# TensorE's products with wq and w3 written as hardware loops of eight turns, in a gated mix of cached attention and an MLP

## The chip, the cores and the metric

The metric is the time of one execution on the device, in microseconds (us), as a median over runs. Lower is better.

## The reference

For two tokens (batch 2, sequence length 1, width D = 1024) it computes `g * a + (1 - g) * b`:

```python
g = sigmoid((x * gate_w).sum(-1, keepdims=True))
# a: attention of one query over a cache of 16384 keys, 32 heads of width 128
q = (x @ wq).reshape(B, 1, 32, 128).transpose(0, 2, 1, 3)
p = softmax(einsum("bhqd,bhkd->bhqk", q, k_cache) * 128 ** -0.5)
a = einsum("bhqk,bhkd->bhqd", p, v_cache).transpose(0, 2, 1, 3).reshape(B, 1, 4096) @ wo
# b: an MLP block; hs is a token-shifted gelu(layernorm(x) @ w1), times w2.
# With one position every shifted copy is zeros; the kernel multiplies zeros with w2.
x1 = x + hs
b = x1 + gelu(layernorm(x1) @ w3) @ w4
```

All operands are bf16. wq is 1024 x 4096, w3 is 1024 x 3584, w4 is 3584 x 1024. The two caches are 2 x 32 x 16384 x 128 each, and make nearly all of the bytes.

## The kernel before

**Planning.** Nothing is issued while the program is written down. `_Plan` (L24) collects for each engine a list of operations with their waits; `add` (L43) appends an operation and, with `sig`, counts the engine's semaphore up by one; `dma` (L52) appends a load. `emit` (L78) then writes each list out in order. It can write a stretch of the list as a hardware loop (`Fori`, L100): the attention part, 32 rounds, becomes 16 turns of two rounds on PE, DVE and ACT. In that loop the value that a wait compares with depends on the turn and is worked out in a register (L72), and one operation per round, the scaled output on DVE (L704), writes to an address from a register.

**Memory.** `ring` has five slots of 128 partitions x 16384 bf16. wq takes slots 0 and 1, w2 slot 2, w3 slots 3 and 4, w4 again 0 and 1 (L352). Round n of the attention takes K into slots 2 and 3 or 3 and 4 (L353), and V into 0 and 1. `queue_load` (L304) lists the loads in a fixed order; `pump` (L307) puts a load on SP's list once its slots have been released, and the load waits for the semaphore values that the release names. SP works its list in order: a small first part of w3, wq, w2, the rest of w3, w4, K of round 0, V of round 0, and so on. `release` (L320) marks a slot free behind an event.

**The start, on PE.** Eight transposes of x and gate_w; the products with wq (L603 to L608): for each of eight blocks of 128 rows (`kc`) 32 products, one for each head, of a 128x128 weight block with a moving operand of two columns, accumulated in bank 1. The first product of a bank clears (`start`), the last of the eight closes. Then four products that spread q (L614), the gate, the products with w2 as rows (L510), `hs_columns`, the layer norm (in turns with DVE and POOL), the products with w3 (L477), the GELU on DVE and ACT, and the products with w4 as rows (L510). Then the loop of the attention, and the products with wo.

**The products with w3.** `dense_stage` (L468) is called eight times (L561), each time with one block `kl` of 128 rows: 28 products of a 128x128 weight block, whose columns lie 28 elements apart (`cols`), with two columns of the normed x. They add up in a zeroed part of bank 5. After the block with which all columns of a slot have been used, the stage releases that slot: slot 3 after the fifth block, slot 4 after the eighth. K of round 0 needs slots 2 and 3, K of round 1 slots 3 and 4.

**What follows from the order.** w4's load waits for the release of wq's slots, K of round 0 for the release of w2's slot and of w3's first, V of round 0 for the release of w4's. Each matmul is a weight load and a product on PE, two instructions, which the text calls a pair.

## Time and profile before

| | us |
|---|---|
| median of three runs | 1324.38 |
| lowest and highest | 1324.28, 1324.6 |
| the profiled execution | 1324.34 |
| its span, first to last instruction | 1323.0 |
| PE busy | 794.4 (60%) |
| DVE busy | 659.9 (50%) |
| TensorE clock granted, mean | 0.78 |

A profile is one execution as the hardware recorded it. The page gives busy times by engine, the span in 40 slices, the DMA queues, the chain of work that ended last, and the costliest groups of instructions. The views behind it are answers to questions about the same record: a timeline of a stretch, the instructions of one line of the code, the waits, the DMA issues. A row of the timeline has start, duration, engine, line, operation, what it writes from what, a count where several are merged, and in brackets how long the engine sat idle before it and what ended that. "issue" stands for a wait that the profile cannot name. SPq is a DMA issue by SP; PEldq and DVEq are instructions that the sequencers of PE and DVE carry out themselves. In the page's part on DMA issues stand KB, and the time from the issue to the landing of the last byte.

### The profile page before, as it was taken

The page shows a single profiled execution, that of the slowest core. Times are in us where ns is not written, and L with a number is a line of the kernel's source. Part 1 is how long each engine was busy: PE and PEld are TensorE (multiplying, and loading weights), DVE is VectorE, ACT ScalarE, POOL GpSimd, SP SyncE. Part 2 cuts the span into 40 slices and gives each one's busy share as a digit, 9 for nine tenths or more (in the row PEclk, how much of TensorE's full clock was granted, in tenths as well). Part 3 has the DMA queues.
Part 4 walks back from the last instruction along what each step waited for, and adds up shares of the span by engine and source line. Part 5 has one row for each costly group of instructions (what it writes and reads, how often), then busy time and mean ns, then how long its engine had stood idle before and what let it go on. Part 6 is the DMA issues. An engine that isn't in the chain of part 4 may idle for free.

```text
span 1323.0 us, 12314 instructions
## 1 busy us (share of the span) xinstructions
PE 794.4 (60%) x5235; PEld 337.7 (26%) x5235; DVE 659.9 (50%) x527; ACT 46.5 (4%) x101; POOL 23.5 (2%) x110
## 2 busy tenths in 40 slices
PE   1655567656556765655676565577565557756557
PEld 1622222212222222222222222222222222222223
DVE  0254446655444665544466554446655445665444
ACT  0000000000000000000000000000000000000000
POOL 3000000000000000000000000000000000000000
PEclk9977778786777877678787767878776787877678
DMA  9999999999999999999999999999999999999998
GB/s 417 433 423 435 436 432 432 436 432 440 428 434 438 428 434 438 430 434 436 430 438 432 430 438 432 430 440 430 430 440 430 430 440 430 430 440 430 430 440 367
DMA packets 11114, 570.60 MB, mean 431 GB/s; under 512 B 1232, under 2 KB 1756, under 8 KB 2015
## 3 DMA queue, kind: packets, MB, share of 16 engines
q1 hardware_dynamic: 11080, 570.43, 99.7%
q8 instruction: 8, 0.13, 0.0%
q14 instruction: 4, 0.02, 0.0%
q10 hardware_dynamic: 22, 0.01, 0.0%
HBM read 570.44 MB, written 0.00 MB: 431 GB/s over the span
## 4 chain that ended last, share of the span: by engine, by line
DMA 69%; PE 24%; DVE 6%; issue 1%; SPq 0%; POOL 0%
DMA ring<-in_A_k_cache_dram 65%; PE ps L654 23%; DVE ring L648 6%; DMA ring<-in_A_wo_dram 2%; DMA ring<-in_A_wq_dram 2%; PE ps L477 1%; PE ps L605 1%; DVE hsd L544 0%; PE ps L510 0%; PE ps L401 0%; SPq L334 0%; PE ps L729 0%; POOL mv L442 0%; DVE orow L763 0%; DVE q_f L617 0%
## 5 line engine op out<-in xcount | busy, mean ns | idle before, releaser
L654 PE MATMUL ps<-ring,Z 128*128 128x512 bf16 x2048 | 534.3, 420 | 375.9 <-DVE ring L648 374.6
L648 DVE STREAM_TRANSPOSE ring<-ring 128x2048 f32<-128x2048 f32 x256 | 565.2, 2274 | 264.6 <-DMA ring<-in_A_k_cache_dram 264.6
L654 PEld LDWEIGHTS ps<-ring,Z 128*128 128x128 bf16 x2048 | 204.2, 104 | 693.2 <-issue 459.3
L690 PE MATMUL ps<-ring,PT_sb 128*32 128x512 bf16 x2048 | 177.4, 523 | 4.3 <-DVE recip L681 3.9
L704 DVE SCALAR_TENSOR_TENSOR OT_sb<-ps,gT,recip 128x2 f32 x32 | 7.0, 220 | 213.0 <-PE ps L701 213.0
L690 PEld LDWEIGHTS ps<-ring,PT_sb 128*32 128x32 bf16 x2048 | 69.6, 126 | 98.4 <-issue 81.7
L675 ACT ACTIVATE P_sb<-ps,negm 128x512 bf16<-128x512 f32 x32 | 22.0, 687 | 995.5 <-DVE negm L673 995.5
L664 DVE TENSOR_REDUCE rA<-ps 128x1 f32<-128x512 f32 x32 | 22.1, 692 | 64.1 <-PE ps L654 64.1
L679 PE MATMUL ps<-rowsum,hsel 128*128 128x1 f32 x128 | 23.9, 291 | 38.0 <-ACT P_sb L675 38.0
L677 DVE STREAM_TRANSPOSE PT_sb<-P_sb 128x512 bf16<-128x512 bf16 x32 | 22.8, 711 | 27.1 <-ACT P_sb L675 27.1
L635 POOL TENSOR_TENSOR Z<-q_f,mask 128x8 bf16<-128x8 f32 x64 | 12.3, 227 | 1204.0 <-PE ps L654 1204.0
L679 PEld LDWEIGHTS ps<-rowsum,hsel 128*128 128x128 f32 x128 | 21.2, 235 | 40.7 <-ACT P_sb L675 40.7
L666 PE MATMUL ps<-ident,rmax_bf 128*1 128x128 bf16 x32 | 6.9, 217 | 33.1 <-DVE rmax_bf L665 33.1
L699 ACT ACTIVATE acc_sb<-ps 128x512 bf16<-128x512 f32 x32 | 19.1, 597 | 208.3 <-PE ps L690 208.3
L701 PE MATMUL ps<-dsel,acc_sb 128*128 128x2 bf16 x128 | 8.1, 167 | 22.5 <-ACT acc_sb L699 22.5
L605 PE MATMUL ps<-xT_bf,ring 128*128 128x2 bf16 x256 | 7.1, 165 | 18.4 <-DMA ring<-in_A_wq_dram 14.1
L477 PE MATMUL ps<-xn_bf,ring 128*128 128x2 bf16 x224 | 14.3, 202 | 1.4 <-DVE xn_bf L444 1.4
L701 PEld LDWEIGHTS ps<-dsel,acc_sb 128*128 128x128 bf16 x128 | 5.3, 96 | 38.3 <-ACT acc_sb L699 38.3
L666 PEld LDWEIGHTS ps<-ident,rmax_bf 128*1 128x1 bf16 x32 | 2.5, 79 | 48.9 <-DVE rmax_bf L665 48.9
L477 PEld LDWEIGHTS ps<-xn_bf,ring 128*128 128x128 bf16 x224 | 14.3, 162 | 1.4 <-issue 1.4
L667 DVE TENSOR_REDUCE m_sb<-ps 1x2 bf16<-1x128 bf16 x32 | 8.9, 279 | 9.9 <-PE ps L666 9.9
L673 DVE TENSOR_SCALAR negm<-ps,cAB 128x1 f32<-128x1 f32 x32 | 8.9, 277 | 9.2 <-PE ps L670 9.2
(99 smaller groups left out, 90.1 us busy)
## 6 DMA issues: line engine op xcount, KB each, us to landing
ring<-in_B_w_dram SPq DMA_DIRECT2D x1, 7168.0 KB, 26.4
ring<-in_B_w_dram SPq DMA_DIRECT2D x1, 6272.0 KB, 43.6
ring<-in_A_wo_dram SPq DMA_DIRECT2D x1, 4096.0 KB, 38.5
ring<-in_B_w_dram SPq DMA_DIRECT2D x1, 2048.0 KB, 28.1
ring<-in_A_wo_dram SPq DMA_DIRECT2D x1, 2048.0 KB, 22.7
ring<-in_A_wo_dram SPq DMA_DIRECT2D x1, 1024.0 KB, 24.8
ring<-in_B_w_dram SPq DMA_DIRECT2D x1, 896.0 KB, 4.6
ring<-in_A_k_cache_dram SPq DMA_DIRECT2D x32, 26.8
```

The costliest lines, as they stand in the source:

```text
L477: fn = lambda e, nb=nb, kl=kl: e.matmul(out_ps[:, nb, :], lhsT=cols(wv, kl, nb, nout), rhs=rhs_of(kl), start=False, stop=True, skip_group_ ...
L605: ev = pl.add("pe", lambda e, h=h, kc=kc: e.matmul(q_ps[:, h, :], lhsT=wv[:, kc, h * Dh:(h + 1) * Dh], rhs=xT_bf[:, kc, :], start=(kc == 0 ...
L635: ev = pl.add("pool", lambda e, hp=hp: e.tensor_tensor(Z[:, :, ZO:ZO + P].rearrange("p t (i c) -> p t i c", c=32)[:, :, 2 * hp:2 * hp + 2, ...
L648: return pl.add("dve", lambda e: e.transpose(ap, ap), waits=(arrived(("k", n)),), sig=True)
L654: ev = pl.add("pe", lambda e, bp=bp: e.matmul(S_ps[:, 0:NCOL], lhsT=Z[:, bp, ZO - 2 * u:ZO - 2 * u + P], rhs=kv[:, :, bp // 2, :, bp % 2], ...
L664: e1 = pl.add("dve", lambda e: e.tensor_reduce(rA[:, :], S_ps[:, 0:NCOL], axis=AX.X, op=ALU.max), waits=(ev_S[n],), sig=True)
L675: e7 = pl.add("act", lambda e: e.activation(P_sb[:, :], S_ps[:, 0:NCOL], ACT.Exp, bias=negm[:, 0:1], scale=scale, accum_out=rowsum[:, 0:1] ...
L677: e8 = pl.add("dve", lambda e: e.transpose(PT_sb[:, :], P_sb[:, :]), waits=(e7,), sig=True)
L679: e9 = pl.add("pe", lambda e, hp=hp: e.matmul(l_ps[:, hp:hp + 1], lhsT=hsel[:, hp, :], rhs=rowsum[:, 0:1], start=True, stop=True, skip_gro ...
L690: ev = pl.add("pe", lambda e, jj=jj, cg=cg: e.matmul(acc_ps[32 * cg:32 * cg + 32, 0:512], lhsT=PT_sb[:, 32 * jj:32 * jj + 32], rhs=vv[:, 4 ...
L699: e1 = pl.add("act", lambda e: e.activation(acc_sb[:, :], acc_ps[:, 0:512], ACT.Copy), waits=(ev_pv,), sig=True)
L701: e2 = pl.add("pe", lambda e, w=w: e.matmul(oT_ps, lhsT=acc_sb[:, w * P:(w + 1) * P], rhs=dsel[:, w, :], start=(w == 0), stop=(w == 3)), w ...
```

## The change

`_Plan` gets a method `turns`, which appends a hardware loop as one entry of an engine's list. Its waits stand ahead of the loop. In the body stand the given operations, which get the turn `i`, and the last of them counts the engine's semaphore up by one each turn; the event that others wait for is the value after the last turn.

```diff
+    def turns(self, eng, count, fns, waits=()):
+        sem = self.esem[eng]
+
+        def fn(e):
+            with e.Fori(0, count) as i:
+                for f in fns:
+                    ins = f(e, i)
+                ins.then_inc(sem, 1)
+
+        self.cnt[eng] += count
+        ev = _Ev(sem, self.cnt[eng])
+        self.ops[eng].append((self._merge(waits), fn, None, 1, False))
+        return ev
```

The products with wq become one such loop: eight turns (over `kc`) of 32 products. The addresses of the weight block and of the moving operand come from a register. As no turn is the first any more in the code, none clears: bank 1's 64 columns are zeroed by DVE before.

```diff
-        for kc in range(NBD):
-            for h in range(H):
-                ev = pl.add("pe", lambda e, h=h, kc=kc: e.matmul(
-                    q_ps[:, h, :], lhsT=wv[:, kc, h * Dh:(h + 1) * Dh], rhs=xT_bf[:, kc, :], start=(kc == 0 and h == 0),
-                    stop=(kc == NBD - 1), skip_group_check=True),
-                    waits=(arrived(key), ev_xT_bf) if h == 0 else (), sig=(h == H - 1))
+        ev_q0 = pl.add("dve", lambda e: e.memset(banks[1][:, 0:H * 2], 0.0), sig=True)
+        ev = pl.turns("pe", NBD, [lambda e, i, h=h: e.matmul(
+            q_ps[:, h, :], lhsT=wv[:, bass.ds(i, 1), h * Dh:(h + 1) * Dh].rearrange("p o d -> p (o d)"),
+            rhs=xT_bf[:, bass.ds(i, 1), :].rearrange("p o b -> p (o b)"), start=False, stop=True, skip_group_check=True)
+            for h in range(H)], waits=(arrived(key), ev_xT_bf, ev_q0))
```

The products with w3 become one loop of eight turns of 28 products. `dense_stage` is called once and releases both slots of w3 behind the last turn.

```diff
-                ev_arr = arrived(key)
-                ev = None
-                first = True
-                for nb in range(nout):
-                    for kl in kls:
-                        lastmm = (nb == nout - 1 and kl == kls[-1])
-                        fn = lambda e, nb=nb, kl=kl: e.matmul(
-                            out_ps[:, nb, :], lhsT=cols(wv, kl, nb, nout), rhs=rhs_of(kl),
-                            start=False, stop=True, skip_group_check=True)
...
-                for j, slot in enumerate(slots_of[key]):
-                    if kls[-1] == _cdiv(min(nkw * width, SLOT * (j + 1)), width) - 1:
-                        release(key, ev, (slot,))
+                fns = [lambda e, i, nb=nb: e.matmul(
+                    out_ps[:, nb, :], lhsT=wv[:, bass.ds(i, 1), :].rearrange("p o (q r) -> p (o q) r", r=nout)[:, :, nb],
+                    rhs=rhs_sb[:, bass.ds(i, 1), :].rearrange("p o b -> p (o b)"), start=False, stop=True, skip_group_check=True)
+                    for nb in range(nout)]
+                ev = pl.turns("pe", nkw, fns, waits=(arrived(key), evd[rhs_key]) + b5_waits())
+                release(key, ev)
...
-        put([dense_stage(key, [kl], NBD, NBF, h3_ps, lambda kc: xn_bf[:, kc, :], "xn2", "h3", F) for kl in range(NBD)], key)
+        put([dense_stage(key, NBD, NBF, h3_ps, xn_bf, "xn2", "h3", F)], key)
```

`b5_waits` gathers the waits that `pe_b5` put ahead of a product into bank 5.

## The prediction

> **What bounds the kernel now.** I read the head of the page and its DMA part first, then the DMA issues, then the chain of waits and the timeline of the first 112 us, and last the rows of the instructions that a sequencer carries out itself.

> ```profile
> span 1323.0 us, 12314 instructions
> DMA  9999999999999999999999999999999999999998
> q1 hardware_dynamic: 11080, 570.43, 99.7%
> HBM read 570.44 MB, written 0.00 MB: 431 GB/s over the span
> ring<-in_B_w_dram SPq DMA_DIRECT2D x1, 7168.0 KB, 26.4
> ring<-in_B_w_dram SPq DMA_DIRECT2D x1, 6272.0 KB, 43.6
> ring<-in_B_w_dram SPq DMA_DIRECT2D x1, 896.0 KB, 4.6
> ```

> The 16 DMA engines work 99.7% of the span. So the time is bytes over 431 GB/s, plus every microsecond in which SP has no load queued. PE matters only through the ring slots that it frees: an earlier free slot is worth nothing while loads are queued, a later one costs all of its lateness beyond the queued work. The place to look at is the start, where the weights pass through the slots:

> ```profile
> 24.93 5.81 PEld L605 LDWEIGHTS ps<-xT_bf,ring 128*128 128x128 bf16 x215 [14.18 <-DMA ring<-in_A_wq_dram]
> 24.94 5.87 PE L605 MATMUL ps<-xT_bf,ring 128*128 128x2 bf16 x214 [14.10 <-DMA ring<-in_A_wq_dram]
> 35.15 1.26 PE L605 MATMUL ps<-xT_bf,ring 128*128 128x2 bf16 x42 [4.34 <-issue]
> 36.44 0.33 SPq L334 DMA_DIRECT2D ring<-in_B_w_dram  x1
> 47.34 14.33 PE L477 MATMUL ps<-xn_bf,ring 128*128 128x2 bf16 x224 [1.35 <-DVE xn_bf L444]
> 56.38 0.33 SPq L361 DMA_DIRECT2D ring<-in_A_k_cache_dram  x1
> 63.77 5.80 PE L510 MATMUL ps<-ring,GT_bf 128*2 128x256 bf16 x112 [2.11 <-DVE GT_bf L462]
> 69.62 0.33 SPq L365 DMA_DIRECT2D ring<-in_A_v_cache_dram  x1
> ```

> Here columns are start, duration, engine, line. wq's products take 24.94 to 36.41, 11.47 us: 7.1 of work and 4.34 in which PE waits for nothing that the profile shows. Their end lets SP issue w4 (36.44). w4 lands 26.4 us later, at 62.8. Its 7168 KB (7.34 MB) need 17.0 us at 431 GB/s, so w3 landed and the queue would have run dry at 62.8 - 17.0 = 45.8. w3's products start 47.34 - 36.41 = 10.9 after the end of wq's and take 14.33; after 140 of 224 SP issues the first K load (56.38). The small load of 896 KB lands after 4.6 us, of which 2.1 are bytes: from an issue to the first bytes 2.5 us. So K's bytes could flow from 58.9, and w4 keeps the engines busy until 62.8: slack 3.9 us. For w4's issue it is 45.8 - 2.5 - 36.4 = 6.9 us.

> **The change, part by part.** The products, their shapes and their bytes stay. In code, 256 and 224 pairs of LDWEIGHTS and MATMUL become 32 and 28, each run eight times. Removed is the 4.34 us gap, if it is what it looks like, waiting for code: one packet of the instruction queue falls into it.

> ```profile
> DMA packets 98, 3.51 MB, mean 438 GB/s; under 512 B 16, under 2 KB 16, under 8 KB 16
> q8 instruction: 1, 0.02, 0.7%
> ```

> (DMA view of 28 to 36 us.) Added are, per turn, the loop's own instructions and, per product, the making of a register address. The trace has both kinds in the main loop: first all such instructions by line, then one back edge.

> ```profile
> L72 PEldq ALU_OP  x416: 32/32/42, 84.5 to 1308.6; - x139
> L72 PEldq FUSED_REGOPS  x48: 37/37/42, 84.4 to 1266.5; - x48
> L72 DVEq ALU_OP  x224: 40/40/52, 102.5 to 1311.3; - x112
> L704 DVEq FUSED_REGOPS  x32: 71/73/81, 111.9 to 1311.4; - x32
> L704 DVE SCALAR_TENSOR_TENSOR OT_sb<-ps,gT,recip x32: 218/220/221, 112.1 to 1311.5; 128x2 f32 x32
> ...
> L100 PEldq ALU_OP  x1: 32/32/32, 150.2 to 150.2; - x1
> L100 PEldq COMPARE_BRANCH  x1: 247/247/247, 150.3 to 150.3; - x1
> L100 PEldq FUSED_REGOPS  x1: 50/50/50, 150.6 to 150.6; - x1
> ```

> A q behind the engine marks its sequencer (ns min/median/max). *Per turn*: from 150.2 to the end of the last, 150.6 + 0.05: 0.45 us.

> *Per product*: at L704 each of 32 operations with a register address has a FUSED_REGOPS of its own, in both halves of the body, so I count one for each of the 32 or 28 weight addresses of a turn (the moving operand's is the same all turn and is made once). What one takes from its sequencer, with the hand-over:

> ```profile
> 43.05 0.05 issue
> 84.39 0.12 issue
> ...
> 111.55 0.25 PE L701 MATMUL ps<-dsel,acc_sb 128*128 128x2 bf16 x4 [0.70 <-ACT acc_sb L699]
> 112.06 0.22 DVE L704 SCALAR_TENSOR_TENSOR OT_sb<-ps,gT,recip 128x2 f32 x1 [6.54 <-PE ps L701]
> ...
> L72 PEldq ALU_OP  x2: 32/32/32, 123.1 to 123.2; - x2
> ```

> The first two are pieces of the chain between the end of a DVE operation and the start of PE's: 0.05 us plain, 0.12 with a 42 ns register instruction between, so 0.07 for that one. On DVE, from PE's end (111.80) to the operation with the address (112.06) pass 0.26 us for two register instructions and the hand-overs. Take off 0.05, and 0.21 is 0.105 each; PE's sequencer does the same ALU_OP in 32 ns where DVE's takes 40 (both at L72), so 0.085. Two register instructions with a group of products between them start 0.1 apart. That bounds the register part between 0.085 and 0.11. The pair itself took 5.87 us / 214 = 0.027 in wq and 14.33/224 = 0.064 in w3, and overlaps in part. **I take p = 0.12 us per product**, between 0.085 (all overlapped) and 0.11 + 0.027 = 0.14 (none).

> W, wq's products: 256 x 0.12 + 8 x 0.45 = 34.3 us (before 11.5). X, w3's: 224 x 0.12 + 3.6 = 30.5 (before 14.3). Both behind data that they wait for, so nothing is done ahead; PE's queue runs empty, as the sequencer is slower than the array.

> On the path: wq's products end at 24.9 + 34.3 = 59.2, w4 is issued then, its bytes flow from 61.7, and the engines stand still from 45.8, **15.9 us**. w4 lands at 61.7 + 17.0 = 78.7. w3's products start at 59.2 + 10.9 = 70.1 and end at 100.6. The release of the first of w3's two slots now comes with that of the last (before after 140 of 224), so K is issued at 100.6, flows from 103.1: the engines stand still from 78.7, another **24.4 us**. In one formula the two are 24.9 + W + 10.9 + X + 2.5 - 62.8 = W + X - 24.5 = 40.3 us, as long as each is above zero.

> What is behind stays hidden: the GELU and w4's rows take until the V issue of 69.62, 8.0 us after w3's products; that gives 108.6, and K's 8.39 MB (128 x 32768 bf16, two slots) keep the engines busy to 122.6. The main loop is bound by its loads (433 GB/s below), so it takes up nothing of a late start. The added memset on DVE (128x64) costs nothing:

> ```profile
> 17.52 0.48 DVE L598 MEMSET ps<- 128x512 f32 x1
> 36.44 0.23 DVE L610 CAST q_sb<-ps 128x64 bf16<-128x64 f32 x1 [18.44 <-PE ps L605]
> ```

> DVE idles from 18.0 on and wq arrives at 24.9; were that cover gone, it would be under the 0.48 of the larger memset. Fewer code packets (q8) are nothing in bytes. The lost early release by itself, with today's 64 ns per product, would be 61.7 + 2.5 - 62.8 = 1.4 us, and the absent gap gives w3's start at most 47.34 - 45.8 = 1.5 back, since w3 lands then.

> The profiled execution took 1324.34 us around its span of 1323.0, as the median of 1324.38. Sum: 1324.3 + 40.3 = **1364.6, say 1365 us**.

> [...] Rows first: the main loop's body on PE is longer than either new one, it turns 16 times, and from 150 us on no packet of PE's instruction queue moves until the end:

> ```profile
> DMA packets 8561, 498.35 MB, mean 433 GB/s; under 512 B 952, under 2 KB 952, under 8 KB 952
> q1 hardware_dynamic: 8560, 498.34, 100.1%
> q14 instruction: 1, 0.01, 0.0%
> ```

> (DMA view of 150 to 1300.) [...]

> **The rivals.**
> - *A: not slower.* Place: PE's sequencer. It makes the next address while the array works, or the addresses are made a turn at a time, so that a product costs at most the 0.027 and 0.064 of today. Then W = 7.1 + 8 x 0.3 = 9.5 and X between 14.3 and 16.7: W + X - 24.5 is between -0.7 and 1.7, nothing is lost, and a surplus is worth nothing: 1324 to 1326. It decides below W + X = 24.5. For: a plain pair at 0.027 us shows that handing out is fast and the array's queue is fed ahead of it. Against: 0.07 us measured for one register instruction, and 480 of them.
> - *A half*: a part of the register work overlaps, p from 0.064 to 0.09: with 0.45 per turn 13 to 26 us more, 1338 to 1350.
> - *B: a weight load or product with a register address is itself handed out by the sequencer.* No row of PE shows one. On DVE the operation at L704 starts 0.06 after its register instruction, as fast as others; but DVE is not PE, whose plain pairs go at 0.027. Priced as two more sequencer instructions of 0.032 (an ALU_OP) to 0.08 us (with hand-over), p is 0.18 to 0.28, in the middle 0.23: 480 x 0.23 + 7.2 - 24.5 = 93 us, 1417. [...]
> [...]

> **How the numbers follow.** Forecast (p from 0.09 to 0.16, 1350 to 1384) 0.55; A half 0.13; A 0.10, a little of it beyond 2.7 us on either side; B 0.18; C 0.04. 0.2% (2.7 us) is about what a measurement of this kernel can tell from no change. Only A can stay within it: same 0.08, faster 0.02, as the DMA engines have no idle time to win back; slower 0.90. The range takes the forecast, most of A half and the lower and middle part of B: 1335 to 1425.

> **What would show it.** Right: rows of PE's sequencer at the new lines, about 480 FUSED_REGOPS or ALU_OP; wq's products over some 34 us and w3's over some 30; an issue of w4 near 59 and of K near 101; DMA slices near zero behind 46 and 79 us; everything after the first K load moved by one amount. Wrong in size: another spacing of the products, which the formula turns into time by 480 us per us. Wrong in kind: wq's products done by 35 us (A), product rows spaced beyond 0.18 with no register instruction between them (B), gaps of microseconds at the back edges with q8 packets in them (C).

## The result, and the profile after

| | before | after |
|---|---|---|
| median, us | 1324.38 | 1370.58 |
| lowest and highest | 1324.28, 1324.6 | 1370.41, 1370.89 |
| profiled execution, and its span | 1324.34, 1323.0 | 1370.52, 1369.2 |

The changed kernel is slower: ratio 1.0349, 95% interval 1.0337 to 1.0361, that is 46.2 us. The forecast was 1365 us, the range 1335 to 1425.

The page of the changed kernel: its first line, and of its second and third part what answers to the lines of before.

```profile
span 1369.2 us, 12845 instructions
...
DMA  9439999999999999999999999999999999999998
GB/s 404 196 136 397 430 431 429 444 437 429 431 433 431 437 444 429 429 433 433 431 440 438 429 431 433 431 433 448 429 429 431 435 429 437 444 429 429 435 431 368
...
q1 hardware_dynamic: 11080, 570.43, 96.5%
q8 instruction: 5, 0.08, 0.0%
```

The bytes are the same; the DMA engines' share fell from 99.7% to 96.5% of a longer span. That is 1319 us of work before and 1321 after: nearly all of the added time is time in which they stand still. One slice is 34 us: the second to fourth have 4, 3 and 9 tenths of DMA, and from the fifth on all is as before. So the whole loss lies ahead of 137 us. In windows of the start (the last two numbers of a row are the DMA engines' busy share and GB/s; a packet is counted whole in the window in which it starts, so a share can be above 1):

```profile
42.00:44.00 2.00, 1.57 (x13) 1.24 (x13) 0.00 (x0) 0.00 (x0) 0.00 (x0) 1.00 0.41 176
44.00:46.00 2.00, 2.00 (x17) 1.62 (x17) 0.00 (x0) 0.00 (x0) 0.00 (x0) 1.00 0.00 0
60.00:62.00 2.00, 1.68 (x16) 1.37 (x15) 0.22 (x1) 0.00 (x0) 0.00 (x0) 1.00 0.00 0
62.00:64.00 2.00, 1.00 (x14) 0.74 (x14) 0.85 (x5) 0.17 (x1) 0.00 (x0) 1.00 1.45 459
80.00:82.00 2.00, 1.56 (x14) 1.48 (x13) 0.00 (x0) 0.00 (x0) 0.00 (x0) 1.00 0.00 0
104.00:106.00 2.00, 1.01 (x8) 0.91 (x8) 0.82 (x5) 0.00 (x0) 0.00 (x0) 1.00 0.00 0
106.00:108.00 2.00, 0.88 (x20) 0.62 (x24) 0.62 (x3) 0.25 (x1) 0.00 (x0) 1.00 1.55 524
```

In two stretches no packet starts: from about 44 to 62 us, ahead of w4's bytes, and from about 80 to 106, ahead of K's. What PE does in them, in the timeline:

```profile
29.85 4.10 PE L612 MATMUL ps<-xT_bf,ring 128*128 x32 [0.50 <-issue]
57.30 4.15 PE L612 MATMUL ps<-xT_bf,ring 128*128 x32 [0.43 <-issue]
72.71 3.77 PE L490 MATMUL ps<-xn_bf,ring 128*128 x28 [1.68 <-DVE xn_bf L463]
76.88 3.67 PE L490 MATMUL ps<-xn_bf,ring 128*128 x28 [0.40 <-issue]
101.35 3.66 PE L490 MATMUL ps<-xn_bf,ring 128*128 x28 [0.43 <-issue]
105.04 0.33 SPq L375 DMA_DIRECT2D ring<-in_A_k_cache_dram  x1
```

From the second turn of wq's products to the eighth pass 27.45 us, 4.575 for a turn of 32 products; for w3's (76.88 to 101.35) 4.08 for a turn of 28. If a product costs the same in both loops, four products make 0.495 us, so **0.124 us for a product and 0.6 for what a turn adds**. The start times in the trace bear it out: in both loops the median distance from one product to the next is 0.124 us. Of the lines of the two loops the sequencer's rows say what fills it:

```profile
L612 PEldq FUSED_REGOPS  x248: 46/46/46, 25.2 to 61.2; - x124
L612 PEldq ALU_OP  x8: 36/36/42, 25.1 to 57.2; - x8
...
L490 PEldq FUSED_REGOPS  x224: 42/46/51, 72.6 to 104.7; - x112
...
L56 PEldq FUSED_REGOPS  x16: 78/78/88, 25.0 to 101.1; - x16
L56 PEldq ALU_OP  x16: 32/34/36, 29.2 to 104.8; - x16
L56 PEldq COMPARE_BRANCH  x16: 76/208/225, 29.3 to 104.9; - x16
```

One register instruction for each of the 480 products, as counted: 248 + 8 for wq, 224 for w3. By the trace's start times the 124 ns of a product are these: 46 ns for the register instruction, 49 ns (48 to 49) from its end to the start of the weight load, and 29 ns (the median in both loops) from there to the next register instruction. The array's own time for a pair, 0.027 us with wq and 0.064 with w3, is not in this sum; it passes meanwhile. And the chain of waits has K's load:

```profile
101.35 3.67 PE ps L490 x28
105.04 23.24 DMA ring<-in_A_k_cache_dram
128.28 0.02 issue
128.31 2.32 DVE ring L655
```

K lands at 128.28, where before it was 82.05: 46.2 us later, the whole of the difference.

### The profile page after: what moved, and what is told of

Read it like the earlier page. It is cut to its first block, busy times and chain, and to the rows that moved or that the text cites. A ratio compares the mean times of both kernels' runs of the same rounds, so it can differ in the third digit from the quotient of the medians.

```text
span 1369.2 us, 12845 instructions
## 1 busy us (share of the span) xinstructions
PE 833.3 (61%) x5235; PEld 371.3 (27%) x5235; DVE 660.0 (48%) x528; ACT 46.5 (3%) x101; POOL 23.6 (2%) x110
## 3 DMA queue, kind: packets, MB, share of 16 engines
q1 hardware_dynamic: 11080, 570.43, 96.5%
HBM read 570.44 MB, written 0.00 MB: 417 GB/s over the span
## 4 chain that ended last, share of the span: by engine, by line
DMA 66%; PE 27%; DVE 6%; issue 1%; SPq 0%; POOL 0%
DMA ring<-in_A_k_cache_dram 63%; PE ps L661 22%; DVE ring L655 5%; PE ps L612 2%; PE ps L490 2%; DMA ring<-in_A_wo_dram 2%; DMA ring<-in_A_wq_dram 2%; DVE hsd L552 0%; PE ps L518 0%; PE ps L420 0%; PE ps L736 0%; SPq L348 0%; POOL mv L461 0%; DVE orow L770 0%; DVE q_f L624 0%
## 5 line engine op out<-in xcount | busy, mean ns | idle before, releaser
L612 PE MATMUL ps<-xT_bf,ring 128*128 x256 | 33.1, 183 | 17.4 <-DMA ring<-in_A_wq_dram 14.3
L612 PEld LDWEIGHTS ps<-xT_bf,ring 128*128 x256 | 26.6, 104 | 23.9 <-issue 17.8
L490 PE MATMUL ps<-xn_bf,ring 128*128 x224 | 29.4, 222 | 4.5 <-issue 2.9
L490 PEld LDWEIGHTS ps<-xn_bf,ring 128*128 x224 | 28.5, 143 | 5.5 <-issue 5.2
## 6 DMA issues: line engine op xcount, KB each, us to landing
ring<-in_B_w_dram SPq DMA_DIRECT2D x1, 7168.0 KB, 21.0
ring<-in_B_w_dram SPq DMA_DIRECT2D x1, 6272.0 KB, 42.4
ring<-in_B_w_dram SPq DMA_DIRECT2D x1, 896.0 KB, 4.6
```

The lines of the kernel that those rows point to most:

```text
L490: fns = [lambda e, i, nb=nb: e.matmul(out_ps[:, nb, :], lhsT=wv[:, bass.ds(i, 1), :].rearrange("p o (q r) -> p (o q) r", r=nout)[:, :, nb] ...
L612: ev = pl.turns("pe", NBD, [lambda e, i, h=h: e.matmul(q_ps[:, h, :], lhsT=wv[:, bass.ds(i, 1), h * Dh:(h + 1) * Dh].rearrange("p o d -> p ...
```

## The experiments

All times are medians; before was 1324.4 beside each of them. Four questions: is it the address or the loop, which part of the address, is the formula of lateness right, and what was the 4.34 us gap that went away.

### Address or loop: every turn with block 0

```diff
-            q_ps[:, h, :], lhsT=wv[:, bass.ds(i, 1), h * Dh:(h + 1) * Dh].rearrange("p o d -> p (o d)"),
-            rhs=xT_bf[:, bass.ds(i, 1), :].rearrange("p o b -> p (o b)"), start=False, stop=True, skip_group_check=True)
+            q_ps[:, h, :], lhsT=wv[:, 0, h * Dh:(h + 1) * Dh],
+            rhs=xT_bf[:, 0, :], start=False, stop=True, skip_group_check=True)
```

and the same for w3 (`cols(wv, 0, nb, nout)` and `rhs_sb[:, 0, :]`).

> Both loops turn eight times, but every turn uses block 0 of the weights and of x: no register address, the same number of products; the sums over the other blocks are left out. Theory: the pairs go back to 0.027 and 0.064 us, a turn costs at most 0.6 more: wq's products take 9 to 12 us, w3's 15 to 19, K is issued between 61.6 and 65.6 and lands 23.2 later: 3 to 7 us over before, 1327 to 1331. Rival (the loop itself, its turns and branches, is what costs): stays above 1355.

Measured: 1326.0 us (ratio 1.0013, interval 1.0001 to 1.0024), a little under the theory's 1327 to 1331, which had K issued at 61.6 to 65.6, and far from the rival. Its timeline:

```profile
25.00 6.96 PE L612 MATMUL ps<-xT_bf,ring 128*128 128x2 bf16 x256 [14.10 <-DMA ring<-in_A_wq_dram]
44.73 14.33 PE L490 MATMUL ps<-xn_bf,ring 128*128 128x2 bf16 x224 [3.18 <-DMA ring<-in_B_w_dram]
59.09 0.33 SPq L375 DMA_DIRECT2D ring<-in_A_k_cache_dram  x1
```

One row each for eight turns, with no idle time inside: 0.027 and 0.064 us a product, those of the code without loops. I had allowed up to 0.6 us a turn; it costs nothing. The sequencer's rows of the loops show why:

```profile
L56 PEldq ALU_OP  x16: 36/36/42, 25.4 to 57.8; - x16
L56 PEldq COMPARE_BRANCH  x16: 76/210/222, 25.5 to 57.9; - x16
```

The first turn's counting starts at 25.4, when the array, at 0.027 us a pair from 25.00 on, has done about half of the turn's 32 pairs. Without register work the sequencer hands out a turn's pairs faster than the array takes them, and counts and branches while the array works off the rest. So the loop itself is free, and it is the address that costs.

### Which part of the address

Two halves. First only the weight's address from a register:

```diff
-            rhs=xT_bf[:, bass.ds(i, 1), :].rearrange("p o b -> p (o b)"), start=False, stop=True, skip_group_check=True)
+            rhs=xT_bf[:, 0, :], start=False, stop=True, skip_group_check=True)
```

> The weight block's address comes from a register as in the changed kernel, the moving operand is block 0 of x in every turn, without a register: the sums use the wrong block of x. Theory 1 (the price is the making of the weight address, once per product): the pairs stay at 0.125 us, 1369 to 1371. Theory 2 (a weight load or a product that reads its address from a register is itself slow to hand out): the product's share goes, some 0.03 us times 480, about 1356.

Measured: 1369.19 us, theory 1's. Then only the moving operand's:

```diff
-            q_ps[:, h, :], lhsT=wv[:, bass.ds(i, 1), h * Dh:(h + 1) * Dh].rearrange("p o d -> p (o d)"),
+            q_ps[:, h, :], lhsT=wv[:, 0, h * Dh:(h + 1) * Dh],
```

> The other half: the moving operand's address comes from a register that is made once a turn, the weight block is block 0 in every turn, without a register: the sums use the wrong weights. Theory 1: no register instruction per product is left, the pairs go back to 0.027 and 0.064 us, 1325 to 1328. Theory 2: the products with a register address stay slow by 0.02 to 0.05 us each, K is issued 8 to 15 us later than that, 1334 to 1341.

Measured: 1325.41 us, again theory 1's. (Both edits were made in w3's loop too.) Third, both operands from registers, but one weight address for all products of a turn:

```diff
-            q_ps[:, h, :], lhsT=wv[:, bass.ds(i, 1), h * Dh:(h + 1) * Dh].rearrange("p o d -> p (o d)"),
+            q_ps[:, h, :], lhsT=wv[:, bass.ds(i, 1), 0:Dh].rearrange("p o d -> p (o d)"),
```

(in w3's loop column 0 instead of `nb`)

> Both addresses come from registers, but all products of a turn use the first weight block of that turn, so one weight address per turn is made instead of 32 or 28; the other columns' products are left out. Theory 1: the pairs go back to 0.027 and 0.064 us although both instructions read registers, 1325 to 1328. Theory 2: of the changed kernel's 0.125 us the 0.078 that are not the register instruction itself stay: K is issued near 83, 1349.

Measured: 1325.34 us, theory 1's once more. The timeline, and the sequencer's rows of wq's line and of the loops:

```profile
25.25 7.95 PE L612 MATMUL ps<-xT_bf,ring 128*128 x256 [14.30 <-DMA ring<-in_A_wq_dram]
44.97 14.35 PE L490 MATMUL ps<-xn_bf,ring 128*128 x224 [2.18 <-DMA ring<-in_B_w_dram]
```

```profile
L612 PEldq ALU_OP  x8: 36/36/42, 25.2 to 32.1; - x8
...
L56 PEldq FUSED_REGOPS  x16: 72/73/88, 25.0 to 56.7; - x16
```

Weight loads and products that read registers go at 7.95 / 256 = 0.031 and 0.064 us a product; the 0.99 us above the 6.96 of the fixed blocks are 0.12 a turn. Reading a register costs nothing to speak of; the time goes with the making of an address, once per product, and in its 46 ns and the 49 ns behind it the sequencer hands out no pair.

### Fewer turns, as many addresses

```diff
-        ev = pl.turns("pe", NBD, [lambda e, i, h=h: e.matmul(
+        ev = pl.turns("pe", 2, [lambda e, i, h=h, k=k: e.matmul(
...
-            for h in range(H)], waits=(arrived(key), ev_xT_bf, ev_q0))
+            for k in range(NBD // 2) for h in range(H)], waits=(arrived(key), ev_xT_bf, ev_q0))
```

with `bass.ds(i * 4 + k, 1)` in both operands; the same in w3's loop.

> The same 480 register addresses in two turns of four blocks each instead of eight turns of one. Theory: 12 back edges fewer at 0.59 us: 7.1 us less than with eight turns, 1363.5, if the address costs the same 0.125 (it has one more step of arithmetic, up to 0.01 more each: up to 1368). Rival (the address's price is spread by the turn, made once per turn): about 1340. [...]

Measured: 1366.87 us, 3.7 less than the changed kernel, inside the theory's range but half of the 7.1 expected from the turns. Of the 0.6 us a turn, the first addresses of a new block are a part, and stay where the block changes inside a turn; how the 0.6 us divides was not measured by itself. The bodies hold 128 and 112 pairs with a register instruction each, and these are the first loop's instructions between its turns:

```profile
L56 PEldq ALU_OP  x1: 32/32/32, 42.5 to 42.5; - x1
L56 PEldq COMPARE_BRANCH  x1: 231/231/231, 42.6 to 42.6; - x1
L56 PEldq FUSED_REGOPS  x1: 83/83/83, 42.9 to 42.9; - x1
```

The branch takes 0.23 us and the turn goes on at once, with its register instruction at 42.9: at this back edge, behind a body of some 390 instructions, no code is waited for.

### One loop at a time

Only w3's products in a loop, wq's as before:

```diff
-        ev_q0 = pl.add("dve", lambda e: e.memset(banks[1][:, 0:H * 2], 0.0), sig=True)
-        ev = pl.turns("pe", NBD, [lambda e, i, h=h: e.matmul(
...
+        for kc in range(NBD):
+            for h in range(H):
+                ev = pl.add("pe", lambda e, h=h, kc=kc: e.matmul(
...
```

> Only w3's products stand in a loop; wq's are written out as before. Theory (480 register addresses at 0.125 us each, and all of the loss sits in the lateness of K's first issue): wq's products end at 36.4 with their 4.34 us gap, w3's take 32.3 and end at 80.0, K is issued there and lands 23.2 us later at 103.2 instead of 82.05: 21 us over before, 1345.5 us. Rival (half of the loss comes from the engines standing still ahead of w4, half ahead of K, and each loop brings its own half): 24.4 of the 40.3, scaled to 46: 28 us, 1352. Rival (the loss comes with any loop, by code fetches at the back edges): gaps of microseconds between the turns.

Measured: 1345.75 us. Only wq's in a loop, `dense_stage` as before:

```diff
-                ev = pl.turns("pe", nkw, fns, waits=(arrived(key), evd[rhs_key]) + b5_waits())
-                release(key, ev)
+                for j, slot in enumerate(slots_of[key]):
+                    if kls[-1] == _cdiv(min(nkw * width, SLOT * (j + 1)), width) - 1:
+                        release(key, ev, (slot,))
```

> Only wq's products stand in a loop; w3's are written out as before, and release slot 3 after 140 of 224. Theory: wq's products end at 61.5, w3's start at 72.4, K is issued after 9.0 us at 81.4, when w4 (landing at 82.5) is just about through: K lands between 101.8 (no break in the stream) and 104.6 (23.2 after its issue), 20 to 23 us over before, 1344 to 1347. With the 21 us of w3's loop alone the two would add up to less than the 46.2 of both, as the late release of slot 3 is in neither sum. Rival (each loop brings its own standstill): 16 of 40.3, scaled 18 us, 1342.

Measured: 1346.95 us. Both lie on the theory's values, and off the rivals' 1352 and 1342. In the chains of waits, first of w3's loop alone and then of wq's alone, K's issue is the start of its row:

```profile
80.22 21.74 DMA ring<-in_A_k_cache_dram
```

```profile
81.58 23.19 DMA ring<-in_A_k_cache_dram
```

Against 56.38 before. The losses, 21.4 and 22.6 us, make 44.0, less than the 46.2 of both. The late release is not the reason, as the expectation had it: w3's loop alone has it too, and is in the sum with it. Each loop by itself first uses up the same slack of before, 2.4 us (worked out below), so in the sum of the two it is taken off twice; 44.0 + 2.4 is 46.4. In w3's loop alone K landed 21.74 us after its issue, where 23.2 had been expected, but the execution was no faster for it: it is K's issue that tells the time, as the table further below shows for all runs.

### The release of slot 3

In the kernel before, the late release alone:

```diff
-                for j, slot in enumerate(slots_of[key]):
-                    if kls[-1] == _cdiv(min(nkw * width, SLOT * (j + 1)), width) - 1:
-                        release(key, ev, (slot,))
+                if kls[-1] == nkw - 1:
+                    release(key, ev)
```

> The kernel before, with both slots of w3 released after the last of its products instead of slot 3 after 140 of 224: nothing else of the change. K is issued at 61.7 instead of 56.4. Theory (K's issue must lie about 4 us ahead of w4's landing at 62.8; it comes 2.9 too late): 3 to 4 us over before, 1327 to 1328.5. Rival (2.5 us from issue to bytes, as in the prediction): 1.4 us over, 1325.8. Rival (the queue has slack for it): 1324.4.

Measured: 1326.79 us (1325.26 to 1327.14; ratio 1.0016, interval 1.0007 to 1.0025), between the theory and the first rival. The profiled execution, of 1325.88 us, tells them apart; its chain:

```profile
2.13 43.69 DMA ring<-in_B_w_dram
45.87 14.37 PE ps L477 x224
60.25 23.24 DMA ring<-in_A_k_cache_dram
```

w3's products began as soon as w3 had landed (45.8), so K was issued at 60.25, not at 61.7 as I had worked out: in this execution the gap in wq's products was 2.43 us instead of 4.34. The eleven times lie in two groups, 1325.3 to 1325.9 and 1326.5 to 1327.1; whether the length of the gap parts them is not shown, as only one execution was profiled. K landed 23.24 us after its issue, at 83.49: 1.44 later than before, and that execution was 1.5 us slower. For no loss K must be issued 23.24 ahead of 82.05, at 58.8, that is 4.0 us ahead of w4's landing, not 2.5. The theory's rule held; the place of the issue was off.

The other way round, the early release given back to the changed kernel by two loops, of five turns and of three:

```diff
-                ev = pl.turns("pe", nkw, fns, waits=(arrived(key), evd[rhs_key]) + b5_waits())
-                release(key, ev)
+                first = _cdiv(SLOT, width)
+                ev = pl.turns("pe", first, fns(0), waits=(arrived(key), evd[rhs_key]) + b5_waits())
+                release(key, ev, slots_of[key][:1])
+                ev = pl.turns("pe", nkw - first, fns(first))
+                release(key, ev, slots_of[key][1:])
```

(`fns(k0)` uses `bass.ds(i + k0, 1)`.)

> The changed kernel with w3's loop cut in two, five turns and three, so that slot 3 is released after 140 of 224 products as before. Theory (K's first issue sets the time): K is issued three turns of 4.08 us earlier, near 92.8, w4 having landed at 82.5; 12 us less than the changed kernel, 1358 to 1359. Rival (the time is set by the whole of w3's products): 1370.5.

Measured: 1358.35 us, 12.2 less than the changed kernel; K is issued at 92.89. The early release that is worth 2.4 us with plain products is worth 12.2 with these, as three turns now last that long.

The profiled executions of all kernels in which K's first issue comes after 58.8 by more than a microsecond lie on one line:

| kernel | K's first issue | profiled execution, us | difference |
|---|---|---|---|
| late release alone | 60.25 | 1325.88 | 1265.6 |
| w3's loop alone | 80.22 | 1345.64 | 1265.4 |
| wq's loop alone | 81.58 | 1347.16 | 1265.6 |
| changed, early release | 92.89 | 1358.38 | 1265.5 |
| two turns | 101.49 | 1367.03 | 1265.5 |
| weight's address alone | 103.73 | 1369.2 | 1265.5 |
| changed | 105.04 | 1370.52 | 1265.5 |

With 1324.34 for the kernel before, the line starts at an issue at 58.8. Close to that point it is not so sharp: the loops with fixed blocks issued K at 59.09 and took 1325.64, those with one address a turn at 59.35 and took 1325.88, each about 1.0 us above the line, and those with the moving operand's address at 59.37 and took 1325.18, 0.3 above it; why is open.

### The gap of 4.34 us

The kernel before, with its eight transposes at the start done seven times over, 48 more pairs of code ahead of wq's products:

```diff
-        for nb in range(NBD):
+        for nb in [n for _ in range(7) for n in range(NBD)]:
             last = pl.add("pe", lambda e, nb=nb: e.transpose(
```

> The kernel before, with its eight transposes at the start done seven times over: 48 more pairs ahead of wq's products, all done before wq arrives. Theory (the 4.34 us gap is TensorE waiting for the next stretch of code, at a fixed place in the code): the gap moves 48 pairs forward, from after product 214 of wq to about 166, with a code packet in it, and the time stays at 1324.4, as w4's issue and K's have slack. Rival (the gap belongs to wq's data or to the array): it stays after product 214.

Measured: 1324.42 us. Its timeline on PE, and its DMA view of 26 to 35 us:

```profile
10.25 3.50 PE L590 MATMUL ps<-ident,xg_row 3*128 3x3 bf16 x56 [10.25 <-DMA xg_row<-in_gate_w_dram]
25.15 4.58 PE L605 MATMUL ps<-xT_bf,ring 128*128 128x2 bf16 x166 [11.41 <-DMA ring<-in_A_wq_dram]
32.97 2.54 PE L605 MATMUL ps<-xT_bf,ring 128*128 128x2 bf16 x90 [3.23 <-issue]
```

```profile
q8 instruction: 1, 0.02, 0.7%
```

The gap stands after product 166 instead of 214, 48 earlier: it is bound to a place in the code, and one packet of code (q8) falls into the 26 to 35 us around it. So the loops did remove a wait for code, and it was worth nothing: the kernel without loops has slack there (here K was issued at 55.47, 0.9 us earlier than before, and the time is the same), and the loops without addresses (above), which have no gap but the late release, are no faster than before.

## Why the prediction was right, by its steps

**What bounds the kernel**: right. The DMA engines are the clock, PE counts only through the slots it frees, and K's landing moved by the whole 46.2 us.

**The register instruction per product**: right in kind and in number, 480. Its price was taken at 0.12 us, a pair with it; it measured 0.124, with 0.6 instead of 0.45 for a turn. The register part, 46 + 49 = 95 ns, lies inside the bounds of 0.085 and 0.11 us. What the forecast left open was how much of the pair overlaps with it: the array's time does entirely, w3's slower pairs cost no more than wq's, but the 29 ns of handing a pair out do not. The 0.12 was chosen between two bounds, 0.085 and 0.14, so that it came within 4% is in part luck. The bounds themselves came from views far from PE's matmuls (one register instruction in the chain between DVE and PE, and one address on DVE), and held. The turn's 0.45 had been read off a back edge whose turn makes no addresses; a new block's first addresses were missing.

**The sum**, term by term, in us:

| term | forecast | measured | from |
|---|---|---|---|
| wq's products after 24.9 | 34.3 | 36.6 | the end at 61.46 |
| from there to w3's products | 10.9 | 11.2 | 72.71 |
| w3's products | 30.5 | 32.3 | 105.04 |
| what the empty queue adds for K | 2.5 | 4.0 | 23.24 less 82.05 - 62.8 |
| sum of them, less 62.8 - 24.9 | 40.3 | 46.2 | |

The end at 61.46 is that of the timeline's row of 57.30 with its 4.15 us. The forecast fell 5.9 us short: 2.3 and 1.8 by the two loops, 0.3 between them, 1.5 by the restart of an empty queue. This last term was also misread. The forecast took the 2.5 us of the first small load as the time from an issue to the first bytes; in the changed kernel w4's and K's first packets start 1.0 us after their issues (none from 105 to 106 us, and K's first from 106.0 on). The 4.0 us are what is lost against a queue that never ran empty: w4, issued into an empty queue, lands after 21.0 us where its bytes need 17.0 at 431 GB/s, and the table of K's issues gives the same 4.0 (62.8 - 58.8). What the other 3 us are no run separates.

**The two standstills**: forecast 15.9 and 24.4 us, with their ends near 62 and 103; seen from about 44 to past 62, and from w4's last packets, which start before 80, to 106. w4 is issued as wq's products end (61.46), and the changed kernel's row for this load in the view of DMA issues has its time to the landing, 21.0 us, so it landed at about 82.5:

```profile
ring<-in_B_w_dram SPq DMA_DIRECT2D x1, 7168.0 KB, 21.0
```

Their lengths needn't add up to the loss, since they are read off the starts of packets in windows of 2 us; K's issue is what counts.

**The late release**: forecast 1.4 us with today's products, measured 2.4. Two errors against each other are in this: 4.0 us instead of 2.5 for the restart, and an issue of K that came earlier than 61.7, by 1.4 us in the profiled execution. With products of 0.124 us it is 12.2, which the formula contained.

**The rivals.** *A*, register work hidden beside the array, fell: the 0.124 us are more than the 46 ns of the register instruction and the 27 ns of a plain pair together. The other 49 ns pass between the register instruction and the weight load behind it; what the sequencer does in them no row names, and the run with one address a turn shows that they go with the making. The condition that it named, though, is real, and the loops with fixed blocks show it: there all of a turn's own work is hidden. *A half* fell with it. *B*, slow handing out of what reads a register, fell by the run with one address a turn, 0.031 us a pair. *C*, code fetched at each back edge and priced at the 4.34 us of the gap, fell: the branches of the 16 back edges took 0.076 to 0.225 us, and no packet of code (q8) starts in either loop (25 to 62 and 72 to 105 us).

**Slack.** The text gave 3.9 us for K's issue; with 4.0 us for the restart it is 2.4 (58.8 - 56.4). It changes nothing of the forecast's side.

## What to carry to other kernels

With 28 or 32 pairs in its body a hardware loop on TensorE is free here, or nearly so (at most 1 us in 256 products), as long as the body's addresses are constants or are made once a turn; an address made for every small product costs more than the product (0.124 us against 0.027). Before shortening code, look whether the engine that reads it has slack in that stage; here a wait for code of 4.34 us was hidden and the addresses, 95 ns a product, were not. Where a load stream bounds the kernel, turn every edit into one number, the time at which the next load can be issued, and keep that early enough for the stream not to break: here 4.0 us ahead of the landing of the last load queued.

## What was not expected of the hardware

- The turn's own work (a branch of up to 0.222 us and a register instruction) vanishes entirely behind 32 pairs of 0.027 us (256 products in 6.96 us).
- A queue of loads that has run empty costs 4.0 us beyond the bytes at 431 GB/s (w4: 21.0 us to the landing for 17.0), though the first packets start 1.0 us after the issue.
- Between a FUSED_REGOPS of 46 ns on PE and the weight load behind it lie 48 to 49 ns, in all 472 of the two loops.
- The branch that closes a loop took 0.23 us on PE even with a body of some 390 instructions (128 pairs with a register instruction each).
